# One core's attention and two MoE layers: the row of maxima ahead of a weight load, the decay rows a place sooner, the gate's weights ahead of the zero rows

## The chip, the cores and the metric

The kernel runs on one core of a Trainium2 chip. The metric is the device time of one execution in microseconds; the time before is the median of three runs. The core has TensorE (matrix products; PE in the profile, PEld for its weight loads), VectorE (DVE), ScalarE (ACT), GpSimd (POOL) and SyncE (SP), which here issues nearly all DMAs. Each engine runs its own queue in order; an instruction that has to wait holds everything behind it on its engine.

## The reference

```python
def _attn_ref(q, k, v, f):                       # (4, 8, 576, 64), f: (4, 8, 576)
    scores = scale * np.matmul(q, k.transpose(0, 1, 3, 2))
    cum = np.cumsum(np.log(np.clip(f, 0.0001, 1.0)), axis=-1)
    decay = cum[:, :, :, None] - cum[:, :, None, :]
    scores = np.where(causal, -1000000000.0, scores + decay)
    scores = scores - np.max(scores, axis=-1, keepdims=True)
    attn = np.exp(scores)
    attn = attn / (np.sum(attn, axis=-1, keepdims=True) + 1e-09)
    return np.matmul(attn, v)

def _moe_ref(x, w1, w2, w3, w_out):              # x: (2304, 512)
    return ((x @ w1) * (x @ w2) @ w3) @ w_out

def _moe2_ref(x, w_gate, w_output_gate, w1, w2): # 8 experts, one for each token
    logits = x @ w_gate
    e_idx = np.argmax(logits, axis=1)
    gate_w = softmax(logits)[np.arange(N), e_idx]
    eom = 1.0 / (1.0 + np.exp(-(x @ w_output_gate)))
    for e in range(E):
        mask = e_idx == e
        h = np.maximum(x[mask] @ w1[e], 0.0)
        out[mask] = gate_w[mask, None] * eom[mask, e, None] * (h @ w2[e])

def reference(**kwargs):
    x = attn(...) as (B * S, H * D)
    return _moe2_ref(_moe_ref(x))
```

## The kernel before

**Attention.** The 32 heads are worked on as 16 pairs (two heads side by side on 128 partitions). For each pair the kernel forms the scores twice. The first time, rows are queries: `scores_of` (tiles `x`, X1 to X3, and `xl` for the last 64 queries) adds the product with the decay rows (`x<-CK,OQ`), and VectorE takes the maximum of each row (`maxima`, line 262) into `M`. TensorE turns `M` (`turn`, line 271), ScalarE copies the result into `mt` (`turned`), and two small DMAs put it as a row into `MR` (`spread_maxima`, lines 276 to 279). The second time, rows are keys: `weights` forms four groups `gA` to `gD` and adds to each the product of the decay rows with the row of maxima (`gA<-MR,CK`); ScalarE takes the exponential into `PT` (`expo`), GpSimd cuts off the masked part and adds blocks (`causal`, `add_blocks`), and `pv` and `sums` multiply with v and form the row sums.

`CK` holds the decay rows of a pair in one of three buffers; `decay` (lines 200 to 207) fills it with two small DMAs, for pairs 0 to 2 from SBUF, from pair 3 on from a copy in DRAM (`EKd`). `MR` has two buffers, the scores' PSUM tiles (`x`, `xl`, `gA` to `gD`) rotate over three.

Beside this, the weights of the first MoE's last two products (`wo` and `w3`, whose product is called Wc) are loaded in pieces of 512 KB, one for each pair (step `c0`, the DMA of `narrow`, line 465), and converted on ScalarE, VectorE and GpSimd in six more steps (`c1`, line 472, is the first to read the piece).

**The order written by hand.** Each step has a name and a start time in `START`; `PERIOD` times the pair's number is added, and `SHIFT` moves single pairs. `attention` sorts all steps by that number and issues them in this order. The numbers are no times of the chip: they only set the order of the instructions on each engine. The steps of the change:

```python
        order = [(START[x] + SHIFT.get((n, x), 0.0) + PERIOD * n, n, i, x) for n in range(B * NP) for i, x in enumerate(START)]
            "ck": (decay,), "qd": (last_queries,), ... "mv": (spread_maxima,),
            stages[f"c{step}"] = (lambda s, step: wc.upto(step, min(s["n"] - 1, EARLY + (2 if step < 2 else 0))), step)
```

SP's queue then repeats a cycle: `kr` (k of a later pair; it waits for VectorE's `kl`), `CK`, `qr`, the sums' store `zd`, `vr`, `QD` (the last queries, wait for ScalarE), the piece `w` or `wo`, `MR`. Some cycles have in addition the inverse row sums (`z`, `rz`, `rb`).

**Behind the attention** come the product Wc, the gated product in five tiles of 512 tokens (`gated`, `project`), and with each tile the routing: `wg` holds the weights of both gates, `lt<-xT,wg` (line 673) is the product with them, and `route` sorts the tokens into `xs` in DRAM, a stretch for each expert. SP writes zero rows into `xs` first (lines 810 to 814, eight DMAs of 771 KB from one tile `zero`) and then loads `wg` (lines 817 to 819). Then the experts follow.

Of the kernel before, what the change touches and what calls it, by code (L numbers as in the profile page):

```python
# [24 lines left out]
N = B * S  # L25
DM = H * D
FF = 1024
E = 8
P = 128
# [3 lines left out]
W = 3 * P  # L33
# [14 lines left out]

PERIOD = 9.8
START = {  # L50
# [8 lines left out]
}  # L59
SHIFT = {(0, "qd"): -2.0, (0, "lq"): 7.41, (0, "lk"): 14.91, (1, "lk"): 15.41, (2, "lk"): 14.9, (3, "lk"): 5.8, (4, "lk"): 2.1, (2, "lq"): 0.5, (0, "kh"): 5.05,  (1, "lq"): 0.5, (0, "XL"): -4.55, (0, "mL"): -5.9, (0, "Tm"): -1.8, (0, "tc"): -1.8, (0, "mv"): -3.49, (1, "Tm"): -0.1, (1, "tc"): -0.1}  # L60

FILL = {(0, "XL"): 10, (1, "X0"): 1, (0, "HA"): 1, (0, "HB"): 3, (1, "XL"): 3, (2, "X0"): 2}

# [13 lines left out]
def attention(nc, tc, ident, xT, rz, xs, wc, q, k, v, f):  # L77
# [7 lines left out]
    with (  # L85
# [314 lines left out]
        for n in range(B * NP):  # L400
            st[n] = {"n": n}
        order = [(START[x] + SHIFT.get((n, x), 0.0) + PERIOD * n, n, i, x) for n in range(B * NP) for i, x in enumerate(START)]
        order = sorted(order + [(t + PERIOD * (B * NP - 1), B * NP, 0, x) for x, t in AFTER.items()])
# [132 lines left out]
def moe(nc, tc, ident, xT, rz, xs, xpool, raws, region, wc, w1, w2, gates, e1, e2, out):  # L536

    V, A, G, PE, SP = nc.vector, nc.scalar, nc.gpsimd, nc.tensor, nc.sync
    NCH = N // P
    with (  # L540
# [269 lines left out]
        zt = wc.work.tile([P, DM + 2], F32, name="zero", tag="raw", bufs=3)  # L810
        G.memset(zt, 0.0)
        G.memset(zt[:, DM + 1:], float(2 * N))
        for e in range(E):
            SP.dma_start(out=xs[e * N:e * N + W].rearrange("(c p) d -> p c d", p=P), in_=zt.unsqueeze(1).broadcast_to([P, W // P, DM + 2]))


        wg = p1.tile([P, 4, 32], F32, name="wg")
        V.memset(wg, 0.0)
        SP.dma_start(out=wg[:, :, :2 * E], in_=gates)
        io = p1.tile([P, E], I32, name="io")  # L820
        G.iota(io, pattern=[[1, E]], base=0, channel_multiplier=0)
        iof = p1.tile([P, E], F32, name="iof")
# [237 lines left out]
        def piece(nm, ws, g, x):  # L1060

            ps = mmt(f"h{nm}")
            for k in range(4):
                for o in range(2):
                    PE.matmul(ps[R * o:R * o + R], x[:, k], ws[0][:, k, 512 * o:512 * o + 512], start=(k == 0), stop=(k == 3))
            rows = p2.tile([P, 512], F32, name=f"hr{nm}", tag="ga")
            for f in (0, 256):
                A.activation(out=rows[:, f:f + 256], in_=ps[:, f:f + 256], func=ACTF.Relu)
            yield
            pt = psx.tile([P, 512], F32, name=f"ht{nm}", tag="x")  # L1070
            for f in range(4):
                PE.transpose(pt[:, P * f:P * f + P], rows[:, P * f:P * f + P], ident)
            pt = pt.rearrange("p (f o c) -> p o f c", f=4, o=2)
            h = pmb.tile([P, 4, WIN[1]], F32, name=f"h{nm}", tag="gxl")[:, :, :2 * R]
            hs = h.rearrange("p (o a) (f c) -> p a o f c", o=2, f=2)
            for a in range(2):
                A.activation(out=hs[:, a], in_=pt[:, :, 2 * a:2 * a + 2], func=ACTF.Copy)
            yield
            ps = mmt(f"o{nm}")[:, :256]
            for f in (0, 1, 4, 5, 2, 3, 6, 7):  # L1080
                for o in range(2):
                    PE.matmul(ps[R * o:R * o + R], h[:, f // 2, R * (f % 2):][:, :R], ws[1][:, f, 256 * o:256 * o + 256], start=(f == 0), stop=(f == 7))
            ot = pmb.tile([P, DM + 2], F32, name=f"ot{nm}", tag="ot", bufs=2)[:, :256]
            A.activation(out=ot, in_=ps, func=ACTF.Copy, scale=g[1])
            G.indirect_dma_start(
                out=out.rearrange("n (t c) -> (n t) c", t=2), out_offset=bass.IndirectOffsetOnAxis(ap=g[2], axis=0),
                in_=ot, in_offset=None, bounds_check=2 * N - 1, oob_is_err=False,
            )
# [57 lines left out]
        with tc.manual_schedule(engines={PE_E, DVE_E}):  # L1146
# [53 lines left out]
            for i in range(1, E):  # L1200
# [28 lines left out]
                else:  # L1229
                    x = turned_piece("p", g2)  # L1230
                    take(y)
                    p = piece("p", ws2, g2, x)
# [8 lines left out]
        with tc.For_i(1, npieces, 1) as s:  # L1241
            e = nc.values_load(tab[0:1, bass.ds(s + E, 1)], engines=SPE, min_val=0, max_val=E - 1)
# [27 lines left out]
def program(shapes):  # L1270
    nc = bacc.Bacc("TRN2", target_bir_lowering=False, num_devices=1)
    a = {n: nc.dram_tensor(n, s, mybir.dt.from_np(t), kind="ExternalInput").ap() for n, (s, t) in shapes.items()}
    out = nc.dram_tensor("out", (N, DM), F32, kind="ExternalOutput").ap()
    with tile.TileContext(nc) as tc:
        with tc.tile_pool(name="keep", bufs=1) as keep, tc.tile_pool(name="raws", bufs=2, reuse_waits="tile") as raws, tc.tile_pool(name="div", bufs=1, space=DRAM) as div:
            rz = div.tile([NP, 2, N], F32, name="rz")

            xs = div.tile([E * N, DM + 2], F32, name="xs")
            ident = keep.tile([P, P], F32, name="ident")
            last = keep.tile([P, 64], F32, name="last")[:, :36]  # L1280
            make_identity(nc, ident)
            xpool = ExitStack()
            xt = xpool.enter_context(tc.tile_pool(name="xt", bufs=1, side="right"))
            xT = xt.tile([P, NP, N], F32, name="xT")
            region = ExitStack()
            region.enter_context(tc.manual_schedule())
            wc = Combined(nc, tc, xpool, raws, a["wo"], a["w3t"], last)
            attention(nc, tc, ident, xT, rz, xs, wc, a["q"], a["k"], a["v"], a["f"])
            moe(nc, tc, ident, xT, rz, xs, xpool, raws, region, wc, a["w1"], a["w2"], a["gates"], a["e1"], a["e2"], out)
            xpool.close()  # L1290
    return nc
# [9 lines left out]
```

## Time and profile before

| | before |
|---|---|
| median of 3 runs (lowest to highest) | 795.74 us (794.42 to 798.16) |
| the profiled execution's own time | 795.65 us |
| its span in the profile | 794.0 us |
| TensorE busy | 770.6 us (97%) |
| VectorE busy | 448.1 us (56%) |
| GpSimd busy | 309.3 us (39%) |
| ScalarE busy | 279.5 us (35%) |
| granted clock of TensorE (mean) | 0.997 |

The profile is one execution of 795.65 us, of which the span of 794.0 us is shown. The attention takes the first 185 us or so, the first MoE's gated product and the routing go to about 555 us, the experts to the end. Busy time is an average over these stages; what a wait is worth is read in its stage. A figure in brackets in a timeline is the idle time of the engine just before the row, with what ended it.

### The profile page before, as it was taken

The numbers are of one execution on the slowest core, as the hardware profiler recorded it, in microseconds if no ns is written. First come the engines' busy times: TensorE is split into PE (matmuls) and PEld (weight loads), VectorE is DVE, ScalarE is ACT, GpSimd is POOL, SyncE is SP. The second block draws the span as 40 slices with busy tenths as digits, with TensorE's granted clock in tenths as the row PEclk, the third lists the DMA queues.
The fourth block names the chain that finished last, engine by engine and source line by source line (L and its number), as shares of the span: only waits on it lengthen the run. The fifth ranks groups of instructions, "written<-read, shape, count | busy, mean of one in ns | idle before, by whom it ended". The sixth has DMA issues, their size and how long they took to land. (4 is left out here: it accounts for less than half of the span.)

```text
span 794.0 us, 13739 instructions
## 1 busy us (share of the span) xinstructions
PE 770.6 (97%) x5126; PEld 639.8 (81%) x5126; DVE 448.1 (56%) x983; ACT 279.5 (35%) x542; POOL 309.3 (39%) x343
## 2 busy tenths in 40 slices
PE   7899989999999999999999999999999999999995
PEld 4577766777888886887888788898797999999983
DVE  7688889988989604332340322337469745545620
ACT  3566656645566222212212221213311222322221
POOL 6588989992000401130230111034444443444510
PEclk9999999999999999999999999999999999999998
DMA  3655445434643191110100000044666556456460
GB/s 91 198 157 154 134 147 163 138 120 147 195 147 137 53 330 58 41 40 14 54 13 7 34 28 0 14 145 149 224 217 221 170 199 224 142 187 213 149 259 30
DMA packets 40211, 102.12 MB, mean 129 GB/s; under 512 B 8610, under 2 KB 9314, under 8 KB 39888
## 3 DMA queue, kind: packets, MB, share of 16 engines
q1 hardware_dynamic: 36960, 91.46, 36.1%
q0 software_dynamic: 3184, 9.77, 3.2%
q8 instruction: 41, 0.67, 0.3%
q14 instruction: 26, 0.21, 0.1%
HBM read 84.47 MB, written 16.51 MB: 127 GB/s over the span
## 5 line engine op out<-in xcount | busy, mean ns | idle before, releaser
L598 DVE TENSOR_TENSOR ga<-b,ga 128x512 f32<-128x512 f32 (+1 forms) x40 | 25.4, 635 | 126.8 <-PE b L570 126.1
L729 POOL DMA_INDIRECT xs<-xr,pos x18 | 19.4, 1076 | 174.6 <-DVE pos L723 128.5
L262 DVE CUSTOM_DVE_ANT_0 junk<-x,tri 128x256 f32<-128x256 f32 (+3 forms) x128 | 62.8, 491 | 17.1 <-PE x L227 7.3
L568 PE MATMUL h<-gh,ah 128*128 128x320 f32 (+4 forms) x224 | 67.2, 300 | 0.0
L569 PE MATMUL h<-gl,ah 128*128 128x320 f32 (+4 forms) x224 | 66.9, 299 | 0.0
L570 PE MATMUL h<-gh,al 128*128 128x320 f32 (+4 forms) x224 | 66.9, 299 | 0.0
L568 PE MATMUL b<-xh,w2h 128*128 128x512 f32 (+1 forms) x160 | 59.9, 375 | 0.0
L568 PE MATMUL a<-xh,w1h 128*128 128x512 f32 (+1 forms) x160 | 59.8, 374 | 0.0
L570 PE MATMUL a<-xh,w1l 128*128 128x512 f32 (+1 forms) x160 | 58.9, 368 | 0.0
L570 PE MATMUL b<-xh,w2l 128*128 128x512 f32 (+1 forms) x160 | 58.9, 368 | 0.0
L569 PE MATMUL a<-xl,w1h 128*128 128x512 f32 (+1 forms) x160 | 58.8, 368 | 0.0
L569 PE MATMUL b<-xl,w2h 128*128 128x512 f32 (+1 forms) x160 | 58.8, 368 | 0.0
L568 PE MATMUL y<-raw,gh 128*128 128x512 f32 x144 | 56.8, 395 | 0.0
L570 PE MATMUL y<-raw,gl 128*128 128x512 f32 x144 | 56.2, 390 | 0.0
L569 PE MATMUL y<-raw,gh 128*128 128x512 f32 x144 | 56.1, 389 | 0.0
L600 ACT ACTIVATE gh<-ga 128x512 fp32r<-128x512 f32 (+1 forms) x40 | 23.6, 590 | 92.1 <-DVE ga L598 92.1
L307 POOL TENSOR_SCALAR_AFFINE_SELECT PT<-PT 128x256 f32<-128x256 f32 (+1 forms) x80 | 43.8, 569 | 26.2 <-ACT PT L301 26.1
L561 POOL TENSOR_SCALAR bh<-rb 128x1024 fp32r<-128x1024 f32 x28 | 34.9, 1248 | 45.7 <-DMA rb<-e 42.1
L1027 DVE SCALAR_TENSOR_TENSOR hl<-h,hh 128x320 fp32r<-128x320 f32 (+4 forms) x56 | 25.4, 462 | 47.7 <-ACT hh L1026 47.1
L584 POOL TENSOR_TENSOR xT<-xT,rz 128x512 f32<-128x512 f32 (+1 forms) x16 | 19.8, 1234 | 77.3 <-ACT w2h L481 77.3
L328 PE MATMUL v<-PT,vr 128*64 128x448 f32 (+4 forms) x384 | 49.8, 396 | 0.0
L319 POOL TENSOR_TENSOR ac<-ac,PT 128x640 f32<-128x640 f32 (+1 forms) x32 | 44.3, 1384 | 1.6
(617 smaller groups left out, 2112.0 us busy)
## 6 DMA issues: line engine op xcount, KB each, us to landing
ra<-e SPq DMA_DIRECT2D x28, 512.0 KB
rb<-e SPq DMA_DIRECT2D x28, 512.0 KB
w<-w3t SPq DMA_DIRECT2D x16, 512.0 KB
xs<-zero SPq DMA_DIRECT2D x8, 771.0 KB
vr<-v SPq DMA_DIRECT2D x16, 320.0 KB
kr<-k SPq DMA_DIRECT2D x16, 288.0 KB
qr<-q SPq DMA_DIRECT2D x16, 288.0 KB
wo<-wo SPq DMA_DIRECT2D x8, 512.0 KB
```

Of the source, the lines that this page charges most:

```text
L262: V.tensor_tensor_reduce(out=junk[:, :w], in0=s["x", i][:, 512 * h:512 * h + w] if i < 4 else s["x", i][:, 224:224 + S], in1=tri[:, 640 - ...
L307: G.affine_select(out=t, in_=t, pattern=[[0, 2], [1, w]], compare_op=ALU.is_ge, fill=0.0, base=0, channel_multiplier=-1,)
L319: G.tensor_tensor(out=acc[:, :, q0 - P:], in0=first if j == 1 else acc[:, :, q0 - P:], in1=src, op=ALU.add)
L328: PE.matmul(s["v"][HALF[h], 384 + q0:384 + q1], s["vr"][:, j, HALF[h]], place(s, j, h, q0, q1), start=(j == 0), stop=(j == 4 or q1 == P),)
L561: G.tensor_scalar(out=hi, in0=src, scalar1=1.0, scalar2=1.0, op0=ALU.mult, op1=ALU.mult)
L568: PE.matmul(ps, ah, bh, start=start and i == 0, stop=False)
L569: PE.matmul(ps, ah, bl, start=False, stop=False)
L570: PE.matmul(ps, al, bh, start=False, stop=stop and i == last)
L584: G.tensor_tensor(out=xv, in0=xv, in1=d, op=ALU.mult)
L598: V.tensor_tensor(out=ga[:, :w], in0=pb[:, :w], in1=ga[:, :w], op=ALU.mult)
L600: A.activation(out=gh[:, f, :w], in_=ga[:, :w], func=ACTF.Copy)
L1027: V.scalar_tensor_tensor(out=hl[:, f, :w], in0=ps[:, :w], scalar=0.0, in1=hh[:, f, :w].bitcast(F32), op0=ALU.max, op1=ALU.subtract)
```

## The change

Three edits of order; no instruction is added or taken away, and none changes its size.

```diff
 PERIOD = 9.8
 START = {
-    "lk": -31.9, "c0": -13.79, "c1": -4.9, "lq": -16.9, "ck": -8.57, "kh": -12.6, "c2": 1.2, "qh": -6.92,
+    "lk": -31.9, "c0": -13.79, "c1": -4.9, "lq": -16.9, "ck": -16.95, "kh": -12.6, "c2": 1.2, "qh": -6.92,
...
-    "kl": 1.21, "XL": 2.1, "mL": 3.54, "Tm": 4.8, "tc": 4.85, "ql": 1.3, "mv": 6.59, "GA": 8.35,
+    "kl": 1.21, "XL": 2.1, "mL": 3.54, "Tm": 4.8, "tc": 4.85, "ql": 1.3, "mv": 5.7, "GA": 8.35,
...
-SHIFT = {(0, "qd"): -2.0, ... (0, "mv"): -3.49, (1, "Tm"): -0.1, (1, "tc"): -0.1}
+SHIFT = {(0, "ck"): 8.38, (1, "ck"): 8.38, (2, "ck"): 8.38, (3, "ck"): 8.38, (0, "qd"): -2.0, ... (0, "mv"): -2.6, (1, "Tm"): -0.1, (1, "tc"): -0.1}
...
-        for e in range(E):
-            SP.dma_start(out=xs[e * N:e * N + W].rearrange("(c p) d -> p c d", p=P), in_=zt.unsqueeze(1).broadcast_to([P, W // P, DM + 2]))
-
-
         wg = p1.tile([P, 4, 32], F32, name="wg")
         V.memset(wg, 0.0)
         SP.dma_start(out=wg[:, :, :2 * E], in_=gates)
+        for e in range(E):
+            SP.dma_start(out=xs[e * N:e * N + W].rearrange("(c p) d -> p c d", p=P), in_=zt.unsqueeze(1).broadcast_to([P, W // P, DM + 2]))
```

`mv` of a pair passes `c0` of two pairs on (both edits of pair 0 cancel out, so pair 0 keeps its place). `ck` of the pairs from 4 on goes 8.38 sooner; pairs 0 to 3 keep their place.

SP's queue in the middle of the attention, one cycle and the beginning of the next (the names end in the pair or the buffer and a running number: `kr_6` is k of pair 6, `CK1` the second of three buffers). Before:

```order
L198 DMA kr_6_591<-k 128x576
L207 DMA CK1_109<-EKd_106 2x576 x2
L198 DMA qr_5_674<-q 128x576
L355 DMA zd_107<-zs_0_627 2x2x288
L198 DMA vr_2_686<-v 128x640
L193 DMA QD0_120<-qh_4_677 64x64 x2
L465 DMA w01_727<-w3t 128x512
L193 DMA MR1_112<-mt_3_717 2x4x128
L193 DMA MR1_112<-mt_3_717 2x1x64
L198 DMA kr_7_745<-k 128x576
L207 DMA CK2_110<-EKd_106 2x576 x2
```

The same place after the change:

```order
L198 DMA kr_6_593<-k 128x576
L207 DMA CK2_110<-EKd_106 2x576 x2
L198 DMA qr_5_676<-q 128x576
L355 DMA zd_107<-zs_0_629 2x2x288
L198 DMA vr_2_688<-v 128x640
L193 DMA QD0_120<-qh_4_679 64x64 x2
L193 DMA MR1_112<-mt_3_719 2x4x128
L193 DMA MR1_112<-mt_3_719 2x1x64
L465 DMA w01_731<-w3t 128x512
L198 DMA kr_7_747<-k 128x576
L207 DMA CK0_108<-EKd_106 2x576 x2
```

`MR` now stands ahead of the piece `w01`, and behind each `kr` stands the `CK` of the pair after the one that stood there (the next buffer of the three), so that at one place, behind `kr` of pair 5, two of them stand in a row. `CK2` behind `kr_6` overwrites the buffer that pair 2 reads last in its `gD`.

SP's queue behind the first tile of the gated product, with `rz` the spread inverse sums, the difference of the two kernels:

```order
 L74 DMA rz12_3473<-rz_63 64x512 x2
 L74 DMA rz13_3479<-rz_63 64x512 x2
-L814 DMA xs_64<-zero_3485 128x3x514 x8
-L819 DMA wg_3496<-gates 128x4x16
+L815 DMA wg_3488<-gates 128x4x16
+L817 DMA xs_64<-zero_3485 128x3x514 x8
 L74 DMA rz20_3980<-rz_63 64x512 x2
 L74 DMA rz21_3986<-rz_63 64x512 x2
```

The gate's weights pass the eight zero rows. The queues of the other four engines hold the same instructions in the same order as before.

## Rows read from the trace of the kernel before

**Rows 1.** Windows by stage: window, its length, then each engine's busy us (count), clock, DMA.

```profile
core 0: us, PE busy (x) PEld busy (x) DVE busy (x) ACT busy (x) POOL busy (x), PEclk, DMA share, GB/s
...
140.00:180.00 40.00, 39.78 (x444) 28.96 (x441) 33.96 (x71) 24.49 (x42) 38.61 (x40) 1.00 0.41 129
180.00:270.00 90.00, 90.00 (x422) 73.40 (x421) 79.31 (x134) 47.52 (x83) 4.88 (x4) 1.00 0.44 147
310.00:520.00 210.00, 209.47 (x1029) 173.11 (x1028) 64.64 (x175) 47.83 (x99) 36.93 (x38) 1.00 0.08 28
```

**Rows 2.** Waits of TensorE, whole span: us in total, times, longest.

```profile
PE gA L227 <- DMA MR<-mt: 3.5, 2, 1.8
PE lt L673 <- DMA wg<-gates: 1.8, 1, 1.8
...
PE x L227 <- DMA CK<-EKd: 1.2, 2, 0.9
```

**Rows 3.** Timeline of TensorE, pairs 0 and 1: start us, us, instruction, [idle before].

```profile
19.02 0.41 PE L227 MATMUL gA<-MR,CK 64*128 64x192 f32 x4
...
31.49 0.51 PE L227 MATMUL gA<-MR,CK 64*128 64x192 f32 x4 [1.79 <-DMA MR<-mt]
...
32.34 0.40 PE L227 MATMUL gC<-qh,kh 64*128 64x448 f32 x3
```

**Rows 4.** Timeline of SP's queue, pairs 0 and 1 (DMA issues).

```profile
16.66 1.14 SPq L193 DMA_DIRECT2D MR<-mt  x2
...
27.59 0.58 SPq L465 DMA_DIRECT2D w<-w3t  x1
28.27 1.16 SPq L193 DMA_DIRECT2D MR<-mt  x2
```

**Rows 5.** Timeline of ScalarE, the turned maxima of pair 1.

```profile
27.19 0.27 ACT L274 ACTIVATE mt<-xl 9x128 fp32r<-9x128 f32 x1 [1.37 <-PE xl L271]
```

**Rows 6.** Timeline of VectorE, the last maxima of pair 2.

```profile
30.86 0.08 DVE L262 DVE_READ_ACCUMULATOR2_ANT M<- 128x1 f32 x1
```

**Rows 7.** Timeline of TensorE, pair 8.

```profile
102.75 0.51 PE L227 MATMUL gA<-MR,CK 64*128 64x192 f32 x4 [1.74 <-DMA MR<-mt]
```

**Rows 8.** Timeline of SP's queue, pair 8.

```profile
97.85 1.18 SPq L193 DMA_DIRECT2D MR<-mt  x2
```

**Rows 9.** Waits of TensorE's weight loads, 40 to 70 us (pairs 2 to 5).

```profile
PEld gA L227 <- DMA MR<-mt: 0.3, 1, 0.3
```

**Rows 10.** Timeline of SP's queue, a cycle without additions (pair 5, up to pair 6's maxima).

```profile
73.03 0.59 SPq L207 DMA_DIRECT2D CK<-EKd  x2
...
75.36 1.17 SPq L193 DMA_DIRECT2D QD<-qh  x2
76.62 0.53 SPq L465 DMA_DIRECT2D wo<-wo  x1
```

**Rows 11.** Timeline of ScalarE, the turned maxima of pair 6 and a piece's conversion.

```profile
77.46 0.27 ACT L274 ACTIVATE mt<-x 9x128 fp32r<-9x128 f32 x1 [1.60 <-issue]
...
87.58 0.68 ACT L472 ACTIVATE wo3u<-wo 128x512 f32<-128x512 f32 x1
```

**Rows 12.** Timeline of TensorE, scores of pair 13 (in pair 12's cycle).

```profile
138.66 0.56 PE L227 MATMUL x<-CK,OQ 64*128 64x256 f32 x2 [0.87 <-DMA CK<-EKd]
```

**Rows 13.** Timeline of VectorE, the same place.

```profile
139.25 0.42 DVE L262 CUSTOM_DVE_ANT_0 junk<-x,tri 128x256 f32<-128x256 f32 x1 [0.60 <-PE x L227]
```

**Rows 14.** Timeline of TensorE, the last reader of pair 5's decay rows.

```profile
73.47 0.31 PE L227 MATMUL gD<-MR,CK 64*128 64x320 f32 x2
```

**Rows 15.** Timeline of SP's queue, zero rows and gate's weights.

```profile
278.02 10.01 SPq L814 DMA_DIRECT2D xs<-zero  x8
288.13 1.78 SPq L819 DMA_DIRECT2D wg<-gates  x1
```

**Rows 16.** Timeline of TensorE, the gate's product and the first matmul of the routing.

```profile
300.20 1.18 PE L673 MATMUL lt<-xT,wg 128*32 128x512 f32 x8 [1.79 <-DMA wg<-gates]
...
310.08 0.19 PE L711 MATMUL rk<-ohb,up 128*128 128x32 bf16 x1
```

**Rows 17.** Timeline of VectorE, the copy that reuses the zero rows' tile.

```profile
300.07 0.21 DVE L726 COPY xr<-tof 128x1 f32<-128x1 f32 x2 [20.23 <-DMA rz<-rz]
```

More of the change, by code (lines that the diff above doesn't have):

```diff
@@ L59 @@
 }
-SHIFT = {(0, "qd"): -2.0, (0, "lq"): 7.41, (0, "lk"): 14.91, (1, "lk"): 15.41, (2, "lk"): 14.9, (3, "lk"): 5.8, (4, "lk"): 2.1, (2, "lq"): 0.5, (0, "kh"): 5.05,  (1, "lq"): 0.5, (0, "XL"): -4.55, (0, "mL"): -5.9, (0, "Tm"): -1.8, (0, "tc"): -1.8, (0, "mv"): -3.49, (1, "Tm"): -0.1, (1, "tc"): -0.1}
+SHIFT = {(0, "ck"): 8.38, (1, "ck"): 8.38, (2, "ck"): 8.38, (3, "ck"): 8.38, (0, "qd"): -2.0, (0, "lq"): 7.41, (0, "lk"): 14.91, (1, "lk"): 15.41, (2, "lk"): 14.9, (3, "lk"): 5.8, (4, "lk"): 2.1, (2, "lq"): 0.5, (0, "kh"): 5.05,  (1, "lq"): 0.5, (0, "XL"): -4.55, (0, "mL"): -5.9, (0, "Tm"): -1.8, (0, "tc"): -1.8, (0, "mv"): -2.6, (1, "Tm"): -0.1, (1, "tc"): -0.1}
 FILL = {(0, "XL"): 10, (1, "X0"): 1, (0, "HA"): 1, (0, "HB"): 3, (1, "XL"): 3, (2, "X0"): 2}
```

## The prediction

> **What bounds the kernel now.** I read the busy time by stage first, then the waits of TensorE, then the timelines of the engines around each wait. By stage [rows 1]: TensorE is busy 39.78 of 40 us, 90.00 of 90 and 209.47 of 210 in the three long stretches shown, at the full granted clock (1.00). It is the bound, and in those stretches every other engine only has to keep up. VectorE and GpSimd come close to not doing so late in the attention: GpSimd is busy 38.61 of the 40 us from 140 to 180.
>
> So a change of order on SP's queue can only save what TensorE waits for. Those waits are few [rows 2]: 3.5 us in two waits for the row of maxima (`MR`), 1.2 us in two waits for the decay rows (`CK`), 1.8 us in one wait for the gate's weights (`wg`). Together 6.5 us of a span of 794.0 us: that is all the change aims at. Since TensorE runs without a gap afterwards, what is saved there should reach the end: the work behind it starts sooner by as much, on all engines that wait for TensorE.
>
> **The row of maxima ahead of the pair's piece.** Two short DMA issues (`MR`) pass one 512 KB load; nothing is added. Cost and gain sit in three pairs.
>
> *Pair 1.* `gA<-MR` started at 31.49 after 1.79 us of waiting [rows 3], so it was wanted at 29.70. SP issued the load at 27.59 and `MR` from 28.27 to 29.43 [rows 4]; it was usable 2.06 us after the issue ended. In pair 0, which has no load ahead, `MR` was issued by 17.80 and read at 19.02 without a wait [rows 3, 4]: at most 1.22 us. The turned maxima were ready at 27.46 [rows 5], so `MR` can go at 27.59 and be issued by 28.75. With 1.22 us it is there at 29.97, a wait of 0.27 instead of 1.79. From `gA<-MR` to the first matmul of `gC` take 32.34 - 31.49 = 0.85 us [rows 3], so `gC` could start at 30.82. But the PSUM buffers of the scores rotate over three, `gC` takes the one in which VectorE still reads the last maxima of pair 2, and that reading ends at 30.94 [rows 6]. So the next thing that is late is VectorE's reading: `gC` starts near 31.0 instead of 32.34, a gain of 1.34. Bounds: 0.68 if the 2.06 us from issue to use stay (28.75 + 2.06 + 0.85 = 31.66), and 1.79 if the reading moves forward too.
>
> *Pair 8.* The wait is 1.74 us, ended at 102.75 [rows 7], so `MR` was wanted at 101.01. It had been issued by 99.03 [rows 8] and took 3.7 us to be usable: there the load and what was queued before it lay ahead. With 1.22 us it is there at 100.25, with 2.06 us at 101.09. Gain 1.74, at least 1.66.
>
> *Pair 4.* Here only the weight load ahead of the matmul waits, 0.3 us [rows 9]. I take 0.2, bounds 0 and 0.3. In the other pairs `MR` is in time, and nothing is gained.
>
> The load itself goes out about 2 us later (it waits until `MR` has gone). It costs nothing: the piece issued at 76.62 is first read by ScalarE at 87.58 [rows 10, 11], 11 us later, so some 8 us of cover remain. If that cover were gone, ScalarE's queue would hold the exponentials of the pair behind it.
>
> A rule of the Trainium skill speaks against the larger gain: its page "DMA: Bandwidth & Descriptors", section "Anatomy of one DMA — SWDGE (gpsimd) path", gives a DMA issued by GpSimd a fixed cost of about 2.0 us, most of it the receipt of the write, whatever its size. If that held for SP's short transfers too, the 2.06 us of pair 1 would be all fixed, and a place ahead of the load would bring only the 0.68 us that SP issues it sooner; pair 0 with at most 1.22 us speaks against it. The case is the first rival below, priced from rows alone.
>
> **Decay rows sooner.** For pairs 4 to 15 the two `CK` copies go one place of the cycle earlier: at the same place of SP's queue (behind `kr`) now stand the rows of the pair after. In pair 12's cycle TensorE waited 0.87 us for them, until 138.66 [rows 12]. But VectorE had been idle only 0.60 us before its next maxima (139.25, [rows 13]): it had its own backlog, and the turning of the maxima waits for it. So of 0.87 about 0.60 comes back. The other wait of the 1.2 us is 0.3; I take the same share, 0.2. Together 0.8; bounds 0.4 (the backlog grows) and 1.2 (all).
>
> What it adds is a wait on TensorE: the buffer is one of three, and now its last reader, the decay product of `gD` of the current pair, is just running. In pair 5's cycle SP issued `CK` at 73.03, while that reader starts at 73.47 and ends about 73.8 [rows 10, 14]. So SP stands 0.8 us, and behind it stand the loads of q and v, the sums, `QD` and `MR` of the next pair. `QD` was issued from 75.36 to 76.53 [rows 10]; 0.8 later it ends at 77.3. `MR` can't go before 77.73 in any case, since the turned maxima are only ready then [rows 11]. The hold fits in with 0.4 us to spare: cost nothing. q and v are wanted most of a cycle later, `QD` in the next cycle.
>
> **The gate's weights ahead of the zero rows.** Before, SP issued the eight zero rows from 278.02 to 288.03 and then the weights from 288.13 to 289.91 [rows 15]; the first matmul on them stood 1.79 us, until 300.20 [rows 16]. Now they go first, as soon as VectorE has cleared their tile; even with the same 1.78 us of issue and 2.06 us more they are there by about 282, while they are wanted at 298.41. Gain 1.79; 1.5 at the least, since a later matmul of this kind can also wait for ScalarE's copies.
>
> The zero rows go out up to 2 us later. VectorE's queue stands until 300.07 behind a copy that reuses their tile [rows 17], so that becomes up to 302. What is queued there is a product of the next tile (`ga`) and then the routing, whose first matmul stands at 310.08 [rows 16], 10 us later, so I cost it at nothing. If that cover were gone, the routing matmuls would wait for VectorE, up to 2 us.
>
> **The sum.** 1.34 + 1.74 + 0.2 + 0.8 + 1.79 = 5.87 us off. The profiled execution took 795.65 us (794.0 of span and 1.65 around it), within 0.1 us of the median of the runs shown, 795.74. 795.65 - 5.87 gives 789.8. The bounds add up to 4.2 (791.4) and 6.8 (788.8).
>
> **Rivals.**
> - *The short transfer's time doesn't depend on the load ahead.* For it: 2.06 us in pair 1. Against: 1.22 us in pair 0, 3.7 us in pair 8. Then pair 1 gives 0.68, pair 8 1.66, pair 4 nothing: 0.68 + 1.66 + 0.8 + 1.79 = 4.9, 790.7 us.
> - *The other engines take it back.* GpSimd is busy 38.61 of 40 us from 140 to 180 [rows 1]; if it, or VectorE with its backlog, sets the pace of pairs 9 to 15, then the 3.3 us of pairs 1, 4 and 8 become waits of TensorE for GpSimd or VectorE. Against: GpSimd's own input comes from the same products, so it starts sooner too. Left are 0.4 and 1.79: 793.5 us.
> - *The zero rows hold VectorE longer than the cover.* The gate's gain is lost, the rest stays: 795.65 - 4.08 = 791.6 us.
> - *Slower: SP's stand at the decay rows.* It comes in 12 pairs. It decides once it is longer than the 0.4 us to spare and the 0.6 us by which `MR` would then land ahead of its use in a normal pair (an estimate from the 1.22 us of pair 0); from there on each us of hold is a us of each pair. One us too much in 12 pairs is 12 us, less the 5.9: 802 us. Against: its end is TensorE's own progress, so the hold can't grow by itself.
>
> **How the numbers follow.** Forecast 0.60 (789.8, own range 788.8 to 791.4), transfer time 0.14 (790.7), taken back 0.14 (793.5), zero rows 0.05 (791.6), slower 0.05 (802), the rest spread. A difference of 0.5% (4 us, at 791.8 and 799.7) is about what a measurement of this kernel tells from no change. Faster by more: the forecast and the first rival, and half of the zero rows, 0.76. Within: 0.19. Slower: 0.05. The range goes from 788.2 to 793.6.
>
> **What would show it.** In the profile after: no wait of TensorE at `gA<-MR` of pair 8, and at most 0.3 to 1.1 us in pair 1, with `gC` of pair 1 waiting for VectorE; none at `x<-CK`; none at the gate's product. SP's `CK` issues released by TensorE, and `MR` still issued within 0.1 us of the turned maxima. TensorE's busy time unchanged and the span shorter by what the waits were. The prediction is wrong if new waits of TensorE for VectorE or GpSimd appear from pair 9 on, or if `MR` is issued late behind `CK`, `v` and `QD`.

## The result, and the profile after

The changed kernel took 789.74 us (median of 10 runs, 788.86 to 790.40) against 796.55 us for the kernel before beside it (10 runs, 792.68 to 799.72): 0.9917 of its time, 95% interval 0.9898 to 0.9936. A second sample on another chip gave 792.93 us against 797.59, 0.9938 (0.9915 to 0.9961), so the gain is 5 to 7 us. The profiled execution took 790.18 us with a span of 788.5, against 795.65 and 794.0. TensorE is busy 769.2 us (98%), before 770.6 (97%); its mean clock is 0.997 in both.

The waits of TensorE in the profile after, whole span: us in total, times, longest.

```profile
...
PE x L271 <- DVE M L262: 1.3, 5, 0.3
PE x L227 <- DVE M L262: 1.1, 3, 0.4
...
PE lg L678 <- ACT lp L675: 0.7, 1, 0.7
...
PE gA L227 <- DMA MR<-mt: 0.2, 1, 0.2
```

The three waits at which the change aimed [rows 2] are gone but for 0.2 us at `gA<-MR`. New are small waits for VectorE's maxima, seven of 0.25 to 0.40 us from pair 10's cycle on, and one of 0.7 us at `lg`, the product that turns the gate's logits. "Before" had two waits for the decay rows and one of 0.2 us for maxima in the same stretch.

The timeline of TensorE after, at the first product with the row of maxima in pairs 0, 1, 8 and 15, and at pair 1's `gC`.

```profile
18.28 0.41 PE L227 MATMUL gA<-MR,CK 64*128 64x192 f32 x4
...
29.17 0.51 PE L227 MATMUL gA<-MR,CK 64*128 64x192 f32 x4 [0.19 <-DMA MR<-mt]
...
30.27 0.50 PE L227 MATMUL gC<-qh,kh 64*128 64x448 f32 x4
...
97.93 0.41 PE L227 MATMUL gA<-MR,CK 64*128 64x192 f32 x4
...
167.47 0.41 PE L227 MATMUL gA<-MR,CK 64*128 64x192 f32 x4
```

The timeline of VectorE after, the last maxima of pair 2:

```profile
30.13 0.08 DVE L262 DVE_READ_ACCUMULATOR2_ANT M<- 128x1 f32 x1
```

The timeline of TensorE before, the same product of pair 15:

```profile
171.88 0.41 PE L227 MATMUL gA<-MR,CK 64*128 64x192 f32 x4
```

Pair 0 starts 0.74 us sooner than in [rows 3]. The change doesn't touch what lies ahead of it, and the gate's edit alone, which leaves the whole attention as it was, has pair 0 at 18.28 too. So 0.74 of the profiles' 5.5 us is no gain of the change. Net of it pair 1's `gC` comes 32.34 - 30.27 - 0.74 = 1.33 us sooner and pair 15 171.88 - 167.47 - 0.74 = 3.67 us sooner.

The timeline of SP's queue after, pairs 1 and 5 and the gate, and below it SP's own waits at `CK` (us in total, times, longest):

```profile
26.89 1.16 SPq L193 DMA_DIRECT2D MR<-mt  x2
28.09 0.39 SPq L465 DMA_DIRECT2D w<-w3t  x1
...
70.47 0.33 SPq L198 DMA_DIRECT2D kr<-k  x1
71.42 0.59 SPq L207 DMA_DIRECT2D CK<-EKd  x2
...
273.90 0.58 SPq L815 DMA_DIRECT2D wg<-gates  x1
274.52 10.44 SPq L817 DMA_DIRECT2D xs<-zero  x8
```

```profile
SPq L207 <- PE gD L227: 6.7, 8, 1.6
```

In pair 1 `MR`'s issue ended at 28.05 and TensorE used the row at 29.17, 1.12 us later. In pair 5's cycle `kr` was done at 70.80 and `CK` went only at 71.42: SP stood some 0.6 us for the decay product of `gD` (0.8 forecast). Over all pairs it stood 6.7 us in 8 places. `MR` of pair 6 was still issued at 75.39, 0.03 us after its turned maxima were ready, as forecast.

The gate after: first TensorE, then VectorE, then ScalarE.

```profile
293.93 1.07 PE L673 MATMUL lt<-xT,wg 128*32 128x512 f32 x8
...
298.69 0.66 PE L678 MATMUL lg<-ident,lp 128*128 128x128 f32 x4 [0.74 <-ACT lp L675]
...
304.67 0.19 PE L711 MATMUL rk<-ohb,up 128*128 128x32 bf16 x1
```

```profile
296.66 0.21 DVE L726 COPY xr<-tof 128x1 f32<-128x1 f32 x2 [21.22 <-DMA rz<-rz]
296.79 0.69 DVE L598 TENSOR_TENSOR ga<-b,ga 128x512 f32<-128x512 f32 x1
```

```profile
297.52 0.63 ACT L600 ACTIVATE gh<-ga 128x512 fp32r<-128x512 f32 x1 [5.48 <-DVE ga L598]
298.06 0.58 ACT L675 ACTIVATE lp<-lt 128x512 f32<-128x512 f32 x1
```

`lt` no longer waits. But VectorE stands until 296.66 at the copy that reuses the zero rows' tile (the bracket names `rz`, which stands behind the zero rows on the same queue; the copy itself needs only the buffer of `zero` and the numbers `tof`); then come its `ga`, ScalarE's `gh` and, behind that on ScalarE's queue, `lp`, for which `lg` waits. Read from VectorE to TensorE, these rows are one chain.

### The profile page after: what moved, and what is told of

It is laid out like the page before. It is cut to its first block, busy times and chain, and to the rows that moved or that the text cites. A ratio compares the mean times of both kernels' runs of the same rounds, so it can differ in the third digit from the quotient of the medians.

```text
span 788.5 us, 13727 instructions
## 1 busy us (share of the span) xinstructions
PE 769.2 (98%) x5126; PEld 637.5 (81%) x5126; DVE 450.0 (57%) x983; ACT 280.4 (36%) x542; POOL 319.9 (41%) x343
## 5 line engine op out<-in xcount | busy, mean ns | idle before, releaser
L598 DVE TENSOR_TENSOR ga<-b,ga 128x512 f32<-128x512 f32 (+1 forms) x40 | 25.4, 635 | 127.2 <-PE b L570 126.5
L561 POOL TENSOR_SCALAR bh<-rb 128x1024 fp32r<-128x1024 f32 x28 | 37.3, 1334 | 45.9 <-DMA rb<-e 42.6
L307 POOL TENSOR_SCALAR_AFFINE_SELECT PT<-PT 128x256 f32<-128x256 f32 (+1 forms) x80 | 47.2, 613 | 18.0 <-ACT PT L301 17.7
```

What stands on the lines that cost most here:

```text
L307: G.affine_select(out=t, in_=t, pattern=[[0, 2], [1, w]], compare_op=ALU.is_ge, fill=0.0, base=0, channel_multiplier=-1,)
L561: G.tensor_scalar(out=hi, in0=src, scalar1=1.0, scalar2=1.0, op0=ALU.mult, op1=ALU.mult)
L598: V.tensor_tensor(out=ga[:, :w], in0=pb[:, :w], in1=ga[:, :w], op=ALU.mult)
```

## The experiments

Unless said otherwise, "before" is the kernel before, run on the same chip, and the interval is of 95%.

**Each edit alone.** The maxima alone, against the kernel before (`SHIFT` of pair 0 keeps its place):

```diff
-"mv": 6.59,  ... (0, "mv"): -3.49
+"mv": 5.7,   ... (0, "mv"): -2.6
```

> Only the row of maxima goes ahead of the piece; the decay rows and the gate's weights stay where they were. Theory A (the place in the queue sets when the row lands): the waits at the maxima of pair 1 (1.79 us) and pair 8 (1.74 us) go, gC of pair 1 waits for VectorE and starts about 1.3 us sooner; the gate's wait of 1.8 us and the decay waits of 1.2 us stay. Some 3.3 us off. Rival (a fixed time from issue to landing): pair 1 gives 0.7 us, pair 4 nothing, some 2.4 us off.

Measured: 793.83 us against 799.11, 0.9937 (0.9915 to 0.9960). Its waits and its pair 15:

```profile
PE lt L673 <- DVE xr L726: 2.5, 1, 2.5
...
PE x L227 <- DMA CK<-EKd: 1.0, 1, 1.0
```

```profile
168.04 0.41 PE L227 MATMUL gA<-MR,CK 64*128 64x192 f32 x4
```

Pair 0 starts at 18.29 here, so pair 15 comes 171.88 - 168.04 - 0.73 = 3.11 us sooner. Theory A, near its 3.3 us. This edit carries most of the gain. One wait for `CK` stays, and the gate's at `lt`: the profile puts it down to VectorE's copy `xr`, which ended in the same moment, but `lt` reads nothing of `xr`; that it waits for the weights is shown further down. The medians differ by more than these rows, 5.3 us; the last section has a possible reason.

The decay rows alone:

```diff
-"ck": -8.57
+"ck": -16.95   SHIFT: + (0, "ck"): 8.38, (1, "ck"): 8.38, (2, "ck"): 8.38, (3, "ck"): 8.38
```

> Only the decay rows go a place sooner. Theory A (VectorE's backlog stands right behind these waits from pair 9 on): the two waits for decay rows go, but TensorE waits for VectorE's maxima in the same pairs, and 0 to 0.5 us come off, most of it in the scores of pair 9. Rival, the forecast's term: 0.8 us off, 0.2 and 0.6 in the cycles of pairs 10 and 12. Rival on the other side (SP's stand at the decay rows): slower by more than 1 us, with the row of maxima issued late.

Measured: 806.66 us, 1.0098 (1.0071 to 1.0125), slower. TensorE's waits for the row of maxima and SP's at `CK`, then SP's queue and TensorE in one cycle:

```profile
PE gA L227 <- DMA MR<-mt: 11.5, 12, 2.1
```

```profile
SPq L207 <- PE gD L227: 25.4, 12, 5.4
```

```profile
53.23 0.34 SPq L198 DMA_DIRECT2D kr<-k  x1
55.24 0.59 SPq L207 DMA_DIRECT2D CK<-EKd  x2
...
58.70 0.53 SPq L465 DMA_DIRECT2D wo<-wo  x1
59.33 1.17 SPq L193 DMA_DIRECT2D MR<-mt  x2
```

```profile
63.51 0.51 PE L227 MATMUL gA<-MR,CK 64*128 64x192 f32 x4 [1.16 <-DMA MR<-mt]
```

SP stands at `CK` from 53.57 to 55.24, until the decay product of `gD` (54.90 to 55.23 on TensorE) has read the buffer. The loads behind it then go out in one bunch, the 512 KB piece ends its issue 0.1 us ahead of `MR`, and `MR` is used 3.01 us after its own issue ended (60.50 to 63.51). From pair 4 on `MR` itself is issued within 0.3 us of the turned maxima; what is late is its transfer. So the rival on the other side is right on the time, but in most pairs not in its way. As these rows read, the waits feed on themselves: a late `MR` makes `gD` late, `gD` holds SP at `CK` longer, and all that stands behind goes out later. SP's stands add up to 25.4 us, against 6.7 in the whole change.

The gate's weights alone (the third piece of the change's diff and nothing else):

> Only the gate's weights go ahead of the zero rows. Theory A: the wait of 1.79 us at the gate's product goes, but the zero rows land about 0.6 us later, VectorE stands that much longer behind its copy, and TensorE waits about 0.7 us at the turning of the gate's result: 1.0 to 1.1 us off. Rival, the forecast's term: 1.79 us off and no new wait.

Measured: 796.25 us, 0.9977 (0.9958 to 0.9995). The wait at `lt` is gone, and a longer one at `lg` for ScalarE's `lp` stands in its place:

```profile
PE lg L678 <- ACT lp L675: 2.4, 1, 2.4
```

Theory A's mechanism, but not its 0.7 us. Counted from pair 15's product with the row of maxima, the routing (`rk`) comes after 138.86 us here and after 138.20 before, so in this profile the gate gave nothing. What the runs gained isn't explained by these rows.

The whole without the decay rows' edit (maxima and gate):

> The change without its decay rows. If they are worth little (theory A), it takes as long as the whole change, at most 0.5 us more, and TensorE's waits for decay rows are back where its waits for VectorE's maxima were. If they are worth the forecast's 0.8 us or more, it is slower by that.

Measured: 792.86 us, 0.9924 (0.9899 to 0.9949). Its pair 15, and its wait at `lg`:

```profile
167.86 0.41 PE L227 MATMUL gA<-MR,CK 64*128 64x192 f32 x4
```

```profile
PE lg L678 <- ACT lp L675: 2.2, 1, 2.2
```

So the decay rows' edit is worth 0.39 us in the whole (167.86 - 167.47), or 0.60 by the second profile of the whole (167.26). Theory A, within 0.1 us of its 0.5. The times can't tell that.

**The whole again, and three variants of it on one chip.** First the changed kernel itself:

> The changed kernel itself, run beside the three variants of it so that they can be compared on one chip. Theory (the forecast's sum, less what the gate gave back): 0.988 to 0.994 of the kernel before, some 790 us where that takes 796; in its profile TensorE waits about 0.7 us at the logits' product lg for ScalarE's lp, 1.0 us in all for decay rows or maxima at most, and the product over VectorE's M at line 271 waits 1 to 1.5 us over some 5 to 8 places. Rival (the first sample was a lucky one): 0.995 or more.

Measured: 792.93 us, 0.9938 (0.9915 to 0.9961). Its wait at `lg` was longer:

```profile
PE lg L678 <- ACT lp L675: 2.0, 1, 2.0
```

The ratio is in the theory's range; the wait is not the 0.7 us that it named. Here the copy behind the zero rows came free at 297.69, 23.38 us after the first zero row's issue at 274.31.

The token numbers on GpSimd, so that VectorE's queue doesn't stand behind the zero rows:

```diff
-                V.tensor_copy(xr[:, DM + 1:DM + 2], tof[:, c0 + c:c0 + c + 1])
+                G.tensor_scalar(out=xr[:, DM + 1:DM + 2], in0=tof[:, c0 + c:c0 + c + 1], scalar1=1.0, scalar2=1.0, op0=ALU.mult, op1=ALU.mult)
```

> The whole change, with the copy of the token numbers into the rows of xr (line 726) done on GpSimd in place of VectorE; the same numbers are written. Theory A (the gate's weights did come sooner, but their gain was partly lost because VectorE's queue stands behind the zero rows at that copy: it came free 22.1 us after the first zero row's issue, as before): VectorE forms ga on time, ScalarE's lp is ready when TensorE gets there, the 0.7 us at lg goes and the time falls by 0.5 to 1.0 us against the whole change, 0.9987 to 0.9993 of it. Rival B (ScalarE itself is late, or GpSimd's own queue is what the gate then waits for): the wait at lg stays, or another of 0.7 us or more takes its place in the gate, and the time is the same or longer by up to 2 us.

Measured: 790.03 us, 0.9908 (0.9889 to 0.9927), span 787.7. VectorE and TensorE in its gate:

```profile
294.00 0.69 DVE L598 TENSOR_TENSOR ga<-b,ga 128x512 f32<-128x512 f32 x1 [18.67 <-PE b L570]
```

```profile
293.82 1.06 PE L673 MATMUL lt<-xT,wg 128*32 128x512 f32 x8
...
297.68 0.60 PE L678 MATMUL lg<-ident,lp 128*128 128x128 f32 x4
...
303.59 0.19 PE L711 MATMUL rk<-ohb,up 128*128 128x32 bf16 x1
```

Theory A holds in its mechanism: `ga` starts at 294.00 as soon as TensorE's `b` is there, and `lg` waits for nothing. The gain is more than its 0.5 to 1.0 us: 1.5 us by the two spans (789.2 and 787.7) and 2.9 by the medians, since the wait at `lg` was 2.0 us in the whole on this chip.

The decay rows right behind the maxima and ahead of the piece:

```diff
-"ck": -16.95 ... (0, "ck"): 8.38, (1, "ck"): 8.38, (2, "ck"): 8.38, (3, "ck"): 8.38
+"ck": -13.85 ... (0, "ck"): 5.28, (1, "ck"): 5.28, (2, "ck"): 5.28, (3, "ck"): 5.28
```

> The whole change, with the decay rows CK issued right behind the row of maxima and ahead of the pair's 512 KB piece, 3.1 us later than in the change and still about 5 us sooner than before. SP then does not stand at CK for TensorE's gD. Theory A (with the maxima ahead of the piece the stand of 0.6 to 1.5 us on SP costs nothing, because all that is behind it is not urgent): same time within 0.1 percent, the waits of TensorE the same. Rival B (the stand still costs, through the maxima's row or the next pair's transfers): 1 to 3 us faster, with less of the 1.0 to 1.5 us that TensorE waits at line 271 and less spacing of the pairs over 9.75 us in pairs 10 to 14.

Measured: 791.88 us, 0.9933 (0.9912 to 0.9953), against 0.9938 for the whole; span 789.4 against 789.2. SP no longer stands for `gD`. Two waits differ: 1.4 us in place of 2.0 at `lg`, and 1.6 in place of 1.0 at `x` for VectorE's maxima. Pair 15 comes at 167.89, no sooner than without the decay rows' edit (167.86), so this place gives up what that edit gains. Theory A as far as the times tell: in the whole change SP's stand costs nothing that can be measured. The stronger sign is that there only one product waits for `MR`, 0.2 us in pair 1, where SP doesn't stand.

Both variants together:

> The whole change with both variants: token numbers copied on GpSimd, and decay rows issued right behind the maxima. Theory: the two touch different stages (gate, attention), so the time is the sum of what each gives alone, 0.998 to 0.9995 of the whole change; the wait of 0.7 us at lg gone, the attention as in the variant with the later decay rows. Rival: GpSimd, which is busy 97 percent in the attention's second half, carries the lateness into the gate, and the time is no better than the whole change's.

Measured: 790.76 us, 0.9919 (0.9899 to 0.9939), span 788.2, no wait at `lg`. That is 0.998 of the whole, in its theory's range, but no better than the token numbers alone.

**The old gate with VectorE free.** The fastest variant (token numbers on GpSimd) with the third edit undone:

```diff
+        for e in range(E):
+            SP.dma_start(out=xs[e * N:e * N + W]...)
         wg = p1.tile([P, 4, 32], F32, name="wg")
         V.memset(wg, 0.0)
         SP.dma_start(out=wg[:, :, :2 * E], in_=gates)
-        for e in range(E):
-            SP.dma_start(out=xs[e * N:e * N + W]...)
```

> The whole change with the token numbers copied on GpSimd as in the fastest variant so far (787.7 us of span, no wait in the gate), but with the third edit undone: the zero rows are issued ahead of the gate's weights again. Theory A (the forecast's: the weights themselves come late when they stand behind the zero rows, whatever VectorE does): TensorE waits again 1.0 to 2.8 us at the gate's first product lt for wg, and the span is 1 to 2.5 us longer than 787.7. Rival B (what was late in the kernel before was in truth VectorE's queue, which stood at the copy until 0.1 us before that product began, and the place of the weights is indifferent): no wait at lt over 0.5 us, span 787.5 to 788.3.

Measured: 794.10 us, 0.9943 (0.9921 to 0.9965), span 790.8. Its waits:

```profile
PE lt L673 <- DMA wg<-gates: 2.5, 1, 2.5
```

Theory A: the weights themselves are late behind the zero rows, whether VectorE is free or not. (The span is 3.1 us longer than 787.7, more than its 1 to 2.5.)

**Where the piece stands when SP is late.** The decay rows alone, with the piece ahead of `QD`:

```diff
-"c0": -13.79
+"c0": -14.9
```

> The decay rows alone (the kernel that took 806.7 us, 1.0098 of the kernel before, with 11.5 us of waits for the row of maxima in 12 pairs), with the pair's 512 KB piece issued ahead of the query rows QD instead of between QD and the row of maxima. SP's stand at CK is the same, so all issues behind it are as late as there. Theory A (the row of maxima is late because the 512 KB piece goes out right ahead of it and lies ahead of it in the DMA queues): with 1.2 us more between the two the waits for the maxima's row fall from 11.5 to under 6 us, time 0.999 to 1.006. Rival B (what matters is that SP itself is late, the place of the piece is indifferent): waits of 9 to 13 us as there, time 1.008 to 1.012.

Measured: 801.93 us, 1.0038 (1.0011 to 1.0066). Its wait:

```profile
PE gA L227 <- DMA MR<-mt: 6.7, 10, 1.3
```

This lies between the two: the time is in theory A's range, the waits (6.7 us) a little over its 6 and under the rival's 9. In the pairs that wait, `MR` is still used 1.6 to 3.1 us after its issue ended (1.8 to 3.8 with the piece right ahead). So some 1.3 us more of distance takes away part of the delay. SP's stands fell with it, from 25.4 to 18.1 us, so the two causes aren't wholly parted. In the runs it is the place behind `MR` that leaves only the 0.2 us of pair 1.

**Why pairs 10 to 14 give something back.** In the profile after, the products of two neighbouring pairs with the row of maxima are 9.75 to 9.79 us apart from pair 3 to pair 9, and then up to 10.7. The whole, with GpSimd's product of the first tile left out:

```diff
-                else:
-                    G.tensor_tensor(out=xT[:, i, 0:512], in0=xT[:, i, 0:512], in1=d, op=ALU.mult)
```

> The whole change with GpSimd's product of the first tile's xT with rb in the attention left out (that tile isn't multiplied, so routing sees other numbers, and only the attention stage is to be read). Theory A (the 0.5 us that pairs 10 to 14 give back, spaced 9.8 to 10.7 us in place of 9.75, come of GpSimd's and VectorE's sharing the work on the pieces there): the spacing of pairs 9 to 13 falls to 9.75 to 9.9 and the start of pair 14 comes 1.5 to 3 us sooner than 155.6. Rival B (VectorE's own work alone sets the pace there): the spacing stays within 0.2 us of 10.7, 10.1, 10.6, 10.1, and pair 14 starts between 155.0 and 155.8.

Measured, pair 15 in its timeline of TensorE (the whole took 800.99 us in one run, which says nothing, since the routing sees other numbers):

```profile
164.87 0.41 PE L227 MATMUL gA<-MR,CK 64*128 64x192 f32 x4
```

All pairs from 3 to 14 are 9.74 to 9.76 us apart, and pair 15 comes 2.60 us sooner than after (167.47). Theory A. How GpSimd holds VectorE can be read in pair 10's cycle: VectorE's `kl` and `ql` in the profile after, then GpSimd beside them.

```profile
107.94 1.84 DVE L220 TENSOR_TENSOR kl<-kr,kh 128x576 fp32r<-128x576 f32 x1
109.71 1.56 DVE L220 TENSOR_TENSOR ql<-qr,qh 128x576 fp32r<-128x576 f32 x1
```

```profile
107.69 1.48 POOL L483 TENSOR_TENSOR raw<-wo3u,raw 128x512 fp32r<-128x512 f32 x1
109.14 1.52 POOL L319 TENSOR_TENSOR ac<-ac,PT 128x384 f32<-128x384 f32 x1
```

The same two of VectorE without the first tile's product, and GpSimd's beside them:

```profile
108.02 1.56 DVE L220 TENSOR_TENSOR kl<-kr,kh 128x576 fp32r<-128x576 f32 x1
109.50 0.96 DVE L220 TENSOR_TENSOR ql<-qr,qh 128x576 fp32r<-128x576 f32 x1
```

```profile
107.77 1.20 POOL L319 TENSOR_TENSOR ac<-ac,PT 128x384 f32<-128x384 f32 x1
...
109.45 1.28 POOL L307 TENSOR_SCALAR_AFFINE_SELECT PT<-PT 128x256 f32<-128x256 f32 x2 [0.48 <-ACT PT L301]
```

An identical subtraction takes 0.96 to 1.84 us; in pair 2's cycle of the profile after, with nothing of GpSimd's beside them, both take 0.75 (39.44 and 40.10). Three of the four end 0.61 us after a GpSimd instruction: 109.78 after `raw`'s end at 109.17, 111.27 after `ac`'s at 110.66, and 109.58 after `ac`'s at 108.97. They look as if they began only when GpSimd had ended. The fourth, 0.96 us long, lies beside GpSimd's cutting off (line 307) and ends before it. GpSimd, 39.28 of 40 us busy from 100 to 140 (before 35.05), is late by the products of the first tile, so its instructions come to lie on `kl` and `ql`, and the maxima behind them come late.

**Giving that product to VectorE.** The fastest variant, and in it:

```diff
-                    G.tensor_tensor(out=xT[:, i, 0:512], in0=xT[:, i, 0:512], in1=d, op=ALU.mult)
+                    V.tensor_tensor(out=xT[:, i, 0:512], in0=xT[:, i, 0:512], in1=d, op=ALU.mult)
```

> The fastest variant so far (the whole change with the token numbers copied on GpSimd, 787.7 us of span), with the first tile's product xT by rb done on VectorE in place of GpSimd; nothing is left out. Theory A (GpSimd, busy 39.3 of 40 us from 100 to 140, makes the pairs 9 to 14 late, since VectorE's subtractions kl and ql end only when GpSimd's instruction beside them has ended): without the four products of 1.29 us on GpSimd the pairs are spaced 9.75 to 9.9 us, the decay product of pair 15 starts at 164.9 to 165.9 us in place of 167.5, and the span is 785.0 to 786.4. Rival B (VectorE itself is the tight engine there, 37.6 of 40 us, and a product of two inputs more, itself behind GpSimd's instruction, takes 0.6 to 1.9 us of it each): the spacing of 10 to 10.7 us stays, that product starts at 167.0 to 169.0, span 787.2 to 789.5.

Measured: 792.94 us, 0.9934 (0.9909 to 0.9958), span 792.2. VectorE's product, GpSimd's instruction beside it, and what TensorE waits for:

```profile
102.82 2.19 DVE L380 TENSOR_TENSOR xT<-xT,rb 128x512 f32<-128x512 f32 x1
```

```profile
102.34 2.11 POOL L319 TENSOR_TENSOR ac<-PT 128x896 f32<-128x896 f32 x1
```

```profile
PE x L271 <- DVE M L262: 5.1, 3, 1.8
```

Rival B, and worse than it said: on VectorE the product takes 2.19 us here and 1.90 to 2.54 in its four places (GpSimd needed 1.29), ending here 0.56 us after GpSimd's `ac` (105.01 and 104.45), and pair 15 comes at 171.29, not at 167.0 to 169.0. Part of that isn't VectorE's: behind these waits, where TensorE was busy for only 0.18 of the 2 us from 104 to 106, its granted clock fell, and pair 9 came 13.1 us after pair 8. The window of TensorE's lower level (window, its length, then busy us of the engines, clock, DMA share, GB/s):

```profile
108.00:110.00 2.00, 2.00 (x26) 1.28 (x22) 1.90 (x10) 0.04 (x1) 1.10 (x2) 0.50 0.56 185
```

The best version found is the whole with the token numbers on GpSimd: 790.03 us beside 792.93 for the whole on the same chip. The intervals of the two ratios overlap; that its wait at `lg` is gone is shown by the profiles.

## Why the prediction was right, point by point

The forecast of 789.8 us and its sum of 5.87 us fit the result (6.8 us by the medians of the first sample, 4.7 by the second). That 789.8 lies 0.06 us from the first median is luck: by the rows, net of pair 0, the first profile is 4.8 us shorter (5.5 - 0.74) and the second 4.1 (794.0 - 789.2 - 0.73), and runs of the kernel before differ by 7 us among themselves. So the forecast holds in the main, by the attention; the gate gave less than its term. By its terms:

- **Pair 1, 1.34 forecast:** 1.33 measured, and by the forecast's path: `MR` came with a wait of 0.19 (0.27 forecast), and `gC` then waited for VectorE (30.27, right behind the reading that ended at 30.21). The upper bound of 1.79 was too wide, since a wait of 0.27 stood in the same working. The rival by which a short transfer takes its 2 us whatever lies ahead is refuted: 1.12 us from the end of issue to use without the load, 3.01 with the load right ahead. The rule of the Trainium skill that was weighed there (page "DMA: Bandwidth & Descriptors", section "Anatomy of one DMA — SWDGE (gpsimd) path") is for GpSimd's DMAs; the 1.12 us (some 1.7 from the start of the second one's issue) show that its 2.0 us don't carry over to these two issued by SP.
- **Pair 8, 1.74 forecast, and pair 4, 0.2:** no wait at either. All of the maxima's edit gave 3.11 us by pair 15 when alone; the three terms say 3.28.
- **Decay rows, 0.8 forecast:** 0.39 and 0.60 by the two profiles of the whole, at the low bound of 0.4. VectorE's backlog takes part of it back, as the step said; what makes the backlog is GpSimd, busy 39.28 of 40 us. So the rival by which the others take it back is true for a small part: from pair 1 to pair 15 the sum says 4.08 us, and 3.67 were left, 3.89 in the second profile. A sign that the prediction had named for its being wrong did come, in small: new waits of TensorE for VectorE from pair 10 on, 2.1 us in all against 0.2 of this kind and 1.2 for decay rows before.
- **SP's stand costs nothing:** right, but the reason given, 0.4 us to spare, isn't enough. Without the maxima's edit the decay rows' edit adds 8 us of waits for `MR` (11.5 against 3.5) and the kernel is slower, 1.0098. With it the stand can't be measured (0.9933 without the stand, 0.9938 with it). The three edits alone multiply to 0.9937 x 1.0098 x 0.9977 = 1.001; together they give 0.992 to 0.994. The first edit is what makes the second one harmless, and the forecast added them up as if they were independent. The fourth rival's mechanism is real while the piece stands ahead of `MR`, and what was held against it, that the hold can't grow by itself, is wrong there: SP's stands grew to 25.4 us, the longest 5.4.
- **Gate, 1.79 forecast:** this term was mis-sized. The step that failed is the one that costs VectorE's stand at the zero rows at nothing, because the routing comes 10 us later. It named `ga` and went on to the routing; but behind `ga` stands ScalarE's `gh`, behind that on the same queue `lp`, and `lg` needs it about 4 us after `lt`. The third rival (the zero rows hold VectorE), given 0.05, is what happened: of the 1.86 us at `lt` it took 0.86 in the first profile and all in the second.

The gate counted from pair 15's product with the row of maxima, worked out from the rows above, [rows 16] and the timelines of these kernels:

| us after that product | `lt` | `lg` | `rk` |
|---|---|---|---|
| before | 128.32 | 132.30 | 138.20 |
| the change, first profile | 126.46 | 131.22 | 137.20 |
| the change, second profile | 126.47 | 132.45 | 138.41 |
| and token numbers on GpSimd | 126.46 | 130.32 | 136.23 |
| the same with the old gate | 129.00 | 132.98 | 138.89 |

`lt` comes 1.86 us sooner (1.79 forecast). By the routing (`rk`) 1.00 us is left in one profile and nothing in the other. With VectorE freed as well, 1.97 us is left, or 2.66 against the old gate with VectorE free. Two waits stood side by side, for the weights and for VectorE, and both ended when the zero rows had drained: the copy came free 22.05 us after the first zero row's issue before [rows 15, 17], 22.14 after, and 23.38 in the second profile of the whole. This drain is 22.05 to 23.80 us long over all profiles that have the copy on VectorE, so a single profile doesn't size the gate's term to better than a us: the wait for the weights itself was 1.79 us before and 2.5 to 2.8 in the other profiles with the old gate. During the drain the 16 DMA engines were busy throughout (mean share 1.04 from 280 to 296 us before, at 366 GB/s). What would shorten it wasn't tried.

## What to carry to other kernels

A short transfer that the bound engine waits for belongs ahead of the long load on its queue. A new wait on that queue cost nothing here only with no long load between it and the short transfer: test edits of one queue together and alone. When a wait is removed, follow the whole chain of the next instruction, over each engine's queue, before calling the cover long; where a second wait ends with the first (here 0.1 us apart), count the gain only up to the second. Work moved off a nearly full engine helps only if the engine that gets it doesn't wait for the first one in turn.

## What the runs showed of the hardware that had not been expected

- **VectorE and GpSimd shut each other out.** VectorE's subtraction of two tiles of 128x576 took 0.75 us alone and 0.96, 1.56 or 1.84 by what GpSimd did beside it, and GpSimd's sum of 128x384 took 1.52 in place of 1.20 us. The Trainium skill says so (page "SBUF — State Buffer", section "Who interferes with whom"): an instruction of VectorE with two inputs in SBUF contends with one of GpSimd that reads SBUF, the ports that they share are an exclusive lock, and the order of issue decides who blocks. The traces agree where GpSimd's instruction is a sum or a product of two tiles: three subtractions end 0.61 us, and a product of 512 columns 0.56 us, behind its end. Beside GpSimd's cutting off (109.45 to 110.73, two instructions) the subtraction of 0.96 us ends 0.27 us ahead of it, so there no such lock to the end is seen.
- **A wait can cost more than its length.** In the whole without the decay edit TensorE stood 2.22 us at `lg`, and the window around it shows a granted clock of 0.79, a mix of its levels of 1.2 and 2.4 GHz. Its four `lg` matmuls took 421 ns each by the median, 273 in the second profile of the whole, and from `lg` to `rk` it took 308.02 - 300.56 = 7.46 us in place of 5.98: 1.5 us on top of the wait. In the second profile of the whole a stand of 1.97 us left the clock at 1.00 in the same window. The window of that first kernel (window, its length, then busy us of the engines, clock, DMA share, GB/s):

```profile
298.00:302.00 4.00, 1.78 (x8) 1.35 (x7) 1.81 (x5) 1.60 (x3) 0.00 (x0) 0.79 0.08 26
```

- **The wait for `MR` in pair 1 can do the same.** In the kernel before it was 1.79 us and the clock stayed at 1.00. With the gate's edit alone, whose attention is that of the kernel before, it was 1.71 us, the window from 32 to 34 us shows 0.50, and pair 2 came 11.40 us after pair 1 in place of 9.86. The prediction has no term for this. It may be why the maxima's edit gained 5.3 us by the medians and 3.1 by its rows: those runs have a mean clock of 0.996 by the median, and the runs of the kernel before beside them 0.992. That isn't shown run by run.
